# An adaLN block with attention on one Trainium2 core: the second query group made first, the modulation rows moved behind

## The chip, the core and the metric

The kernel runs on one core of a Trainium2 chip. The metric is the device time of one execution in microseconds (us); lower is better. The core has a matrix engine (TensorE, PE below), a vector engine (VectorE, DVE), a scalar engine (ScalarE, ACT), a general engine (GpSimd, POOL), an engine that starts transfers (SyncE, SP), and queues for transfers (DMA). Each engine works off its own list of instructions in order; where one needs another engine's result, it waits on a semaphore.

## What is computed

The sequence has 2048 rows of 512 columns. There are 32 heads of 16 columns for the queries, and one key and one value head that all of them share.

```python
def _A_ref(x, wq, wk, wv, wo):
    q = (x @ wq).reshape(B, S, H, Dh).transpose(0, 2, 1, 3)
    k, v = x @ wk, x @ wv
    scores = jnp.einsum("bhqd,bkd->bhqk", q, k) * (Dh ** -0.5)
    o = jnp.einsum("bhqk,bkd->bhqd", softmax(scores), v)
    return o.transpose(0, 2, 1, 3).reshape(B, S, H * Dh) @ wo

x = A_x
sa, ca, ga, sb, cb, gb = split_in_six(silu(c) @ w_mod)
h = layernorm(x) * (1 + ca) + sa
x = x + ga * _A_ref(h, A_wq, A_wk, A_wv, A_wo)
h = layernorm(x) * (1 + cb) + sb
x = x + gb * (gelu(h @ w1 + b1) @ w2 + b2)        # 1376 columns in between
```

Everything is float32, and the result must be close to float32 products. The kernel therefore splits each operand into a high part (fp32r, a type that PE multiplies in one pass) and the remainder as a low part, and makes three products for one: high by high, low by high and high by low.

## The kernel before

The rows are worked in four blocks of 512. For a block the prologue takes the statistics of the rows (`stats1`), normalizes them on ACT (`xhat1`, L362), turns each of four column parts of 128 with PE's transposes into a tile `tp` (`turn1`, L371), applies scale and shift on ACT (`mod1`, L377) and splits the result into `h0H`/`h0L` for block 0 and `big1H`/`big1L` to `big3H`/`big3L` for the others (L134 or L132 the high, L139 the low part). These four steps of a column part are called a head of the block below. Then come the products for keys and values, `kps` (L164, twelve of them, since there are four column parts k and three products each); ACT copies the keys into `ks` (L392) and the values into `vt` (L393), DVE makes the keys' low part (`low_k`, L398), ACT repeats it on other partitions (`repeat_k`, L402), and PE turns the values (`v_out`, `vps`, L410).

Queries come in four groups of 128 columns. `prep_wq(g)` splits the weight of group g, in two halves j of the columns, into the tiles `wqH` and `wqL`, each of which holds all 512 columns of the four parts k (ACT's copy L334, POOL's subtraction L335). `qproj(b, g)` makes the group's twelve products `qps` (mm3, L164), three for each k, takes the high and low part out of them and sends both to memory (`send_q`, L415); `load_q(u)` (L487 and L488) reads them back in another layout into a tile `qst`, for a unit u of the attention. Group 0 of block 0 feeds the units 0 and 1, group 1 the units 2 and 3.

The softmax needs the maximum of each row of scores first. `Max.step` makes a product m of `qst` and `ks` on PE (L517), 512 keys wide, and DVE reduces it (L522). A unit has 32 of these products in four sets of keys kc, and the table FIRST_MAX says in which order the sets of the units 0 and 1 are taken: set kc can be made when block kc's keys are ready. When the last reduction of unit 0 is done, `put_max` reduces over the sets (`mm`, L571), turns the result (L572), gathers it on POOL (`mt`, L566), splits it, and transfers it into rows of `qst` (L561). Then the first product e of unit 0 runs (L597), the second product of the same scores, now less the maximum, then the exponential on ACT (L598) and the products with the values (L609).

The order of the code is the order on each engine. In the prologue's last part it is set by the table SLOTS: each entry makes so many max products and then one step of each piece of work that it names ("keys 1" is one k of block 1's key products, "heads 2" a head of block 2, "low 1" `low_k` of block 1, "k 1" `repeat_k`, "v 0" `v_out`, "q 1" a k of group 1's projection, "wq 1" `prep_wq(1)`, "rows" a fourth of the late modulation rows `modl`, L289, and "load" the query loads of unit 2). The rest of the modulation (`modr`) is made at the start. Past the table a loop makes the attention, one unit behind the other; the order from the first e on is set by the planner that is not touched here. While the projection of group 0 is made, `stats1(2)` runs on DVE, and a function `first_q` that is called between its parts makes the projection.

## Times and profile before

| | us |
|---|---|
| median of three runs (1581.46 to 1582.77) | 1582.67 |
| the profiled execution | 1580.99 |
| its span, first to last instruction | 1579.2 |
| PE busy in it | 1556.4 |
| DVE busy | 1405.5 |
| ACT busy | 1204.6 |
| POOL busy | 694.9 |
| the first max product of unit 0 | 33.16 |
| the first product e of unit 0 | 78.47 |

The span is the time from the first instruction to the last, and the profiled execution's own time lies 1.8 above it. Busy time is a sum over all stages; which stage an engine limits is seen in a timeline. A line of a timeline has the start and the duration of an instruction or of a run of equal ones ("x3"), its engine, line, operation and tiles (out<-in), and in brackets the idle time before it and what ended it. The granted clock (PEclk) is a share of 2.4 GHz: 1.00 is 2.4 GHz, 0.50 is 1.2 GHz.

### The profile page before, as it was taken

Reading aid. Unit: us, or ns where it says so; the run is one execution under the profiler, and the core shown is the slowest. Engines: PE = TensorE matmul, PEld = TensorE weight load, DVE = VectorE, ACT = ScalarE, POOL = GpSimd, SP = SyncE. Lnnn points to the kernel's source line nnn. Section 1 sums busy time; section 2 is a strip of 40 time slices with the busy share of each in tenths; the row PEclk is TensorE's granted clock in tenths of the full one; section 3 lists DMA queues with packets and bytes.
Section 4 is the critical chain, followed back from the end, with each engine's and each line's share of the span. In section 5 each row is a group of like instructions: output and inputs, shape, how many; then the busy total and the mean of one; then the engine's idle time right before and its main releaser. Section 6 shows DMA issues by size and latency. Waiting matters only on the chain.

```text
span 1579.2 us, 43484 instructions
## 1 busy us (share of the span) xinstructions
PE 1556.4 (99%) x17514; PEld 1040.6 (66%) x17514; DVE 1405.5 (89%) x2491; ACT 1204.6 (76%) x2418; POOL 694.9 (44%) x1253
## 2 busy tenths in 40 slices
PE   5999999999999999999999999999999999999999
PEld 3466655667766676667766676666766677676767
DVE  7899999999999999999999999999999999999715
ACT  5577777788777887778877887778877788778853
POOL 4445457447422472245623363334712464324731
PEclk8999999999999999999999999999999999999999
DMA  7135322313021220302112120212112130221231
GB/s 261 73 108 205 118 83 89 99 44 97 21 61 62 64 78 21 101 25 95 45 54 72 45 98 20 92 33 85 56 36 89 36 109 22 60 80 50 96 141 54
DMA packets 80859, 121.48 MB, mean 77 GB/s; under 512 B 16187, under 2 KB 55355, under 8 KB 80401
## 3 DMA queue, kind: packets, MB, share of 16 engines
q1 hardware_dynamic: 80640, 118.70, 23.1%
q8 instruction: 137, 2.24, 0.6%
q14 instruction: 66, 0.53, 0.1%
q10 hardware_dynamic: 16, 0.00, 0.0%
HBM read 91.00 MB, written 26.88 MB: 75 GB/s over the span
## 4 chain that ended last, share of the span: by engine, by line
PE 95%; ACT 3%; DVE 1%; DMA 1%; issue 0%; POOL 0%; SPq 0%; DVEq 0%; ACTq 0%
PE acc L609 32%; PE e L597 20%; PE m L517 19%; PE w1ps L193 8%; PE w2ps L193 6%; PE wops L193 3%; PE qps L193 2%; ACT p L598 2%; PE w2ps L187 1%; PE w1ps L187 1%; DMA xt<-in_A_x_dram 1%; PE tp L193 1%; PE kps L164 1%; DVE mx L522 1%; PE wops L187 0%
## 5 line engine op out<-in xcount | busy, mean ns | idle before, releaser
L522 DVE TENSOR_REDUCE mx<-m 128x1 f32<-128x512 f32 x2048 | 1271.5, 682 | 98.2 <-PE m L517 87.4
L598 ACT ACTIVATE p<-e 128x512 f32<-128x512 f32 x2048 | 1067.2, 601 | 291.5 <-PE e L597 204.2
L517 PE MATMUL m<-ks,qst 64*128 64x512 f32 x2048 | 829.2, 432 | 6.0 <-DVE mv L203 4.6
L597 PE MATMUL e<-qst,ks 64*128 64x512 f32 x2048 | 731.8, 412 | 2.1 <-ACT wqH L334 1.3
L609 PE MATMUL acc<-p,va 128*32 128x256 f32 x8192 | 548.8, 385 | 0.0
L517 PEld LDWEIGHTS m<-ks,qst 64*128 64x128 f32 x2048 | 367.3, 184 | 103.2 <-DVE mx L522 83.5
L597 PEld LDWEIGHTS e<-qst,ks 64*128 64x128 f32 x2048 | 357.7, 184 | 112.6 <-ACT p L598 102.0
L609 PEld LDWEIGHTS acc<-p,va 128*32 128x32 f32 x8192 | 214.0, 109 | 217.6 <-issue 113.9
L193 PE MATMUL w1ps<-h2H,w1t 64*128 64x256 f32 x1232 | 236.2, 288 | 0.0
L193 PEld LDWEIGHTS w1ps<-h2H,w1t 64*128 64x128 f32 x1232 | 184.0, 184 | 31.7 <-issue 22.2
L566 POOL TENSOR_SCALAR mt<-turned 8x32 f32<-8x32 f32 x256 | 53.1, 208 | 342.1 <-DVE turned L572 330.0
L193 PE MATMUL w1ps<-h2L,w1t 64*128 64x256 f32 x616 | 169.3, 275 | 0.0
L193 PE MATMUL w2ps<-w2H,gH 64*128 64x256 f32 (+1 forms) x556 | 162.2, 296 | 0.0
L193 PE MATMUL w2ps<-w2L,gH 64*128 64x256 f32 (+1 forms) x556 | 156.5, 283 | 0.0
L193 PE MATMUL w2ps<-w2H,gL 64*128 64x256 f32 (+1 forms) x556 | 155.1, 283 | 0.0
L193 PEld LDWEIGHTS w1ps<-h2L,w1t 64*128 64x128 f32 x616 | 113.5, 184 | 0.0
L193 PEld LDWEIGHTS w2ps<-w2H,gH 64*128 64x128 f32 x556 | 101.6, 184 | 10.7 <-issue 4.9
L193 PEld LDWEIGHTS w2ps<-w2H,gL 64*128 64x128 f32 x556 | 101.8, 184 | 2.3
L193 PEld LDWEIGHTS w2ps<-w2L,gH 64*128 64x128 f32 x556 | 102.4, 184 | 1.2
L965 POOL TENSOR_SCALAR tt<-tt 128x256 f32<-128x256 f32 x77 | 31.0, 403 | 145.1 <-ACT tt L964 144.8
L193 PE MATMUL wops<-woH,onH 64*128 64x256 f32 x224 | 67.9, 303 | 0.0
L193 PE MATMUL wops<-woL,onH 64*128 64x256 f32 x224 | 62.2, 278 | 0.0
(235 smaller groups left out, 1604.6 us busy)
## 6 DMA issues: line engine op xcount, KB each, us to landing
w1t<-dw SPq DMA_DIRECT2D x82, 512.0 KB
qst<-dq SPq DMA_DIRECT2D x128, 64.0 KB
do<-oc SPq DMA_DIRECT2D x63, 128.0 KB
dw<-w1s SPq DMA_DIRECT2D x11, 512.0 KB
xt<-in_A_x_dram SPq DMA_DIRECT2D x4, 1024.0 KB
dq<-qH SPq DMA_DIRECT2D x16, 256.0 KB
dq<-qL SPq DMA_DIRECT2D x16, 256.0 KB
qst<-dq SPq DMA_DIRECT2D x128, 32.0 KB
```

The costliest lines, as they stand in the source:

```text
L164: nc.tensor.matmul(ps, a, b_, start=begin and n == 0, stop=end and n == last)
L187: nc.tensor.matmul(ps, a, b_, start=first_, stop=last_)
L193: nc.tensor.matmul(ps, a[rows], b_[rows], start=first_ and s == begin, stop=last_ and s != begin)
L517: nc.tensor.matmul(m, qsts[u][rows, j, t * P:(t + 1) * P], ks[rows, kc * 512:(kc + 1) * 512], start=True, stop=True)
L522: nc.vector.tensor_reduce(out=self.mx[u][:, i, kc:kc + 1], in_=m, axis=AX.X, op=ALU.max)
L566: nc.gpsimd.tensor_scalar(out=mt[:, g:g + 32], in0=turned[g:g + 4 * T, :], scalar1=1.0, scalar2=0.0, op0=ALU.mult, op1=ALU.add)
L597: nc.tensor.matmul(e, ks[rows, kt * P:(kt + 1) * P], rhs, start=True, stop=True)
L598: nc.scalar.activation(ptiles[u, K][:, j, s, :], e, AF.Exp, scale=0.25)
L609: ins = nc.tensor.matmul(accs[u][32 * cidx:32 * cidx + 32, :], va[:, kt, :], rhs, start=kt == 0, stop=kt == NKT - 1)
L965: nc.gpsimd.tensor_scalar(out=tt, in0=tt, scalar1=1.0, scalar2=1.0, op0=ALU.mult, op1=ALU.add)
```

## The change

`prep_wq` takes an engine for the high part, and now leaves the split to `split`: group 0 goes as before, by ACT and POOL, while for the groups 1 to 3 both parts are made on POOL (a TENSOR_SCALAR, L132, and the subtraction, L139, for each half). `prep_wq(1)` is called right after the first two instructions of block 1's normalizing, ahead of `first_q` in the code. Group 1's projection (`q_group`) is called behind `repeat_k(0)`, ahead of the normalizing of blocks 2 and 3 and of the first max product. In SLOTS the weights of groups 2 and 3 are made at other places, the steps of "q 1" are gone, the first step of "keys 3", which had no max products with it, has two, and the four parts of "rows" stand in the last four entries with "load" in the first of these; "v 2" and "v 3" have entries with two max products each, and two entries have max products alone.

```diff
 SLOTS = (...,
-         (2, "low 2", "k 2", "v 1", "wq 1"), (0, "keys 3"), (2, "keys 3"), (2, "keys 3"), (2, "keys 3"), (2, "low 3", "k 3"),
-         (0, "v 2"), (2, "q 1"), (2, "q 1"), (2, "q 1"),
-         (2, "q 1", "rows"), (2, "v 3", "load", "wq 2", "wq 3"), (2, "rows"), (2, "rows"), (2, "rows"))
+         (2, "low 2", "k 2", "v 1", "wq 2"), (2, "keys 3"), (2, "keys 3"), (2, "keys 3"), (2, "keys 3", "wq 3"), (2, "low 3", "k 3"),
+         (2, "v 2"), (2, "v 3"), (2, ), (2, ),
+         (2, "rows", "load"), (2, "rows"), (2, "rows"), (2, "rows"))
...
-    def prep_wq(g):
+    def prep_wq(g, eng=nc.gpsimd):
         gs = slice(g * P, (g + 1) * P)
         for j in range(2):
...
-            nc.scalar.copy(dh, src)
-            nc.gpsimd.tensor_tensor(out=dl, in0=src, in1=raw(dh), op=ALU.subtract)
+            split(dh, dl, src, eng, nc.gpsimd)
...
-    prep_wq(0)
+    prep_wq(0, act)
...
     rows = xhat1(1, act)
     run(rows, 2)
+    prep_wq(1)
...
     repeat_k(0)
+    run(q_group())
     run(xhat1(2, act))
     run(xhat1(3, act))
-    work = {..., "q 1": q_group(), ..., "wq 1": one(prep_wq, 1), "wq 2": one(prep_wq, 2), "wq 3": one(prep_wq, 3)}
+    work = {..., "wq 2": one(prep_wq, 2), "wq 3": one(prep_wq, 3)}
```

On PE, the beginning of group 0's projection in the program before; the brackets name the engines whose semaphores the instruction waits for:

```order
L164 MATMUL qps_0_314<-h0H,wqH 128x512 [waits Activation_49]
L164 MATMUL qps_0_314<-h0H,wqL 128x512 [waits Pool_49]
L164 MATMUL qps_0_314<-h0L,wqH 128x512 [waits Pool_49]
L164 MATMUL qps_0_314<-h0H,wqH 128x512 [waits Pool_49]
L164 MATMUL qps_0_314<-h0H,wqL 128x512
L164 MATMUL qps_0_314<-h0L,wqH 128x512 [waits DVE_49]
```

The same place on PE in the program after:

```order
L164 MATMUL qps_0_318<-h0H,wqH 128x512 [waits Activation_49]
L164 MATMUL qps_0_318<-h0H,wqL 128x512 [waits Pool_49]
L164 MATMUL qps_0_318<-h0L,wqH 128x512 [waits Pool_49]
L164 MATMUL qps_0_318<-h0H,wqH 128x512 [waits Pool_49]
L164 MATMUL qps_0_318<-h0H,wqL 128x512 [waits Pool_49]
L164 MATMUL qps_0_318<-h0L,wqH 128x512 [waits DVE_49]
```

The products and their order are the same; the fifth, which had no wait, has one for POOL.

On POOL, from the low part of block 0's first column part on, in the program before:

```order
L139 TENSOR_TENSOR h0L<-h_0_0_258,h0H 128x512 [waits Activation_49]
L132 TENSOR_SCALAR h0H<-h_0_1_275 128x512 [waits Activation_49]
L207 TENSOR_TENSOR rs<-ve,mhalf 128x4 [waits DVE_49]
L352 TENSOR_TENSOR nm_292<-mv,rs 128x4 [waits Pool_49]
L353 TENSOR_SCALAR nm_292<-nm_292 128x4 [waits Pool_49]
L266 MEMSET b1c 128x1
L207 TENSOR_TENSOR rs<-ve,mhalf 128x4 [waits DVE_49]
```

The same stretch of POOL in the program after:

```order
L207 TENSOR_TENSOR rs<-ve,mhalf 128x4 [waits DVE_49]
L351 TENSOR_TENSOR nm_292<-mv,rs 128x4 [waits Pool_49]
L352 TENSOR_SCALAR nm_292<-nm_292 128x4 [waits Pool_49]
L266 MEMSET b1c 128x1
L132 TENSOR_SCALAR wqH<-wqf 128x4x64 [waits DMAHW2_49]
L139 TENSOR_TENSOR wqL<-wqf,wqH 128x4x64 [waits Pool_49]
L132 TENSOR_SCALAR wqH<-wqf 128x4x64
L139 TENSOR_TENSOR wqL<-wqf,wqH 128x4x64 [waits Pool_49]
L207 TENSOR_TENSOR rs<-ve,mhalf 128x4 [waits DVE_49]
```

The four instructions of group 1's split stand between the memset of `b1c` and the statistics of block 2.

On ACT, from the last head of block 1 to the copy of block 1's keys, in the program before:

```order
L134 CAST big1H<-h_1_3_420 128x512 [waits Activation_49]
L402 CAST ks<-ks 16x512 [waits DVE_49]
L362 ACTIVATE xt_148<-xt_148,nm_351,rs 128x512 [waits DMAHW3_49,Pool_49]
L362 ACTIVATE xt_148<-xt_148,nm_351,rs 128x512 x3
L362 ACTIVATE xt_151<-xt_151,nm_432,rs 128x512 [waits DMAHW5_49,DVE_49,Pool_49]
L362 ACTIVATE xt_151<-xt_151,nm_432,rs 128x512 [waits DVE_49] x3
L392 CAST ks<-kps_459 48x512 [waits PE_49]
```

The same stretch of ACT in the program after:

```order
L134 CAST big1H<-h_1_3_424 128x512 [waits Activation_49]
L401 CAST ks<-ks 16x512 [waits DVE_49]
L440 COPY q_0_1_457<-qps_1_442 128x512 [waits PE_49,Pool_49]
L134 CAST qH_1_455<-q_0_1_457 128x512 [waits Activation_49]
L361 ACTIVATE xt_148<-xt_148,nm_355,rs 128x512 [waits DMAHW3_49]
L361 ACTIVATE xt_148<-xt_148,nm_355,rs 128x512 x3
L361 ACTIVATE xt_151<-xt_151,nm_436,rs 128x512 [waits DMAHW5_49,DVE_49,Pool_49]
L361 ACTIVATE xt_151<-xt_151,nm_436,rs 128x512 [waits DVE_49] x3
L391 CAST ks<-kps_484 48x512 [waits PE_49]
```

The copy and the cast of group 1's query stand ahead of the normalizing of blocks 2 and 3.

## Rows read from the trace of the kernel before

**Rows 1.** The page: the span, and the chain that ended last, by engine.

```profile
span 1579.2 us, 43484 instructions
...
PE 95%; ACT 3%; DVE 1%; DMA 1%; issue 0%; POOL 0%; SPq 0%; DVEq 0%; ACTq 0%
```

**Rows 2.** Timeline of PE, 18.5 to 38 us: start, duration, engine, line, operation.

```profile
19.00 0.50 PE L164 MATMUL qps<-h0L,wqH 128*128 128x512 f32 x1
19.59 0.50 PE L164 MATMUL qps<-h0H,wqH 128*128 128x512 f32 x1
...
24.56 0.39 PE L164 MATMUL kps<-h0L,wkH 128*128 128x512 f32 x1
...
33.16 1.19 PE L517 MATMUL m<-ks,qst 64*128 64x512 f32 x3 [4.57 <-DVE mv L203]
...
35.43 0.79 PE L164 MATMUL kps<-big1H,wkH 128*128 128x512 f32 x1
...
36.87 0.63 PE L164 MATMUL kps<-big1H,wkH 128*128 128x512 f32 x1
37.30 0.63 PE L164 MATMUL kps<-big1H,wkL 128*128 128x512 f32 x1
```

**Rows 3.** Timeline of SP's queue, 20 to 30 us.

```profile
24.77 0.34 SPq L415 DMA_DIRECT2D dq<-qL  x1
```

**Rows 4.** Busy time of engines by half microsecond; the granted clock stands behind POOL.

```profile
29.50:30.00 0.50, 0.00 (x0) 0.00 (x0) 0.50 (x2) 0.47 (x2) 0.50 (x2) 0.71 0.35 107
30.00:30.50 0.50, 0.00 (x0) 0.00 (x0) 0.30 (x1) 0.50 (x2) 0.47 (x1) 0.50 0.13 41
39.00:39.50 0.50, 0.50 (x3) 0.49 (x2) 0.39 (x1) 0.00 (x0) 0.00 (x0) 0.50 0.97 393
...
40.00:40.50 0.50, 0.50 (x4) 0.42 (x3) 0.40 (x1) 0.00 (x0) 0.00 (x0) 1.00 1.18 483
```

**Rows 5.** Timeline of ACT, 21 to 46; a group of 0 to 80.

```profile
23.45 0.56 ACT L437 CAST qH<-qps 128x512 fp32r<-128x512 f32 x1
...
25.33 1.16 ACT L392 CAST ks<-kps 48x512 fp32r<-48x512 f32 x2
...
31.88 0.62 ACT L402 CAST ks<-ks 16x512 fp32r<-16x512 f32 x1
32.53 5.75 ACT L362 ACTIVATE xt<-xt,nm,rs 128x512 f32<-128x512 f32 x8
41.12 1.17 ACT L392 CAST ks<-kps 48x512 fp32r<-48x512 f32 x2 [2.85 <-PE kps L164]
...
L441 ACT COPY q<-qps 128x512 f32<-128x512 f32 x1 | 0.6, 585 | 4.1 <-PE qps L164 4.1
```

**Rows 6.** Timeline of DVE, 24 to 46 us.

```profile
33.96 2.48 DVE L522 TENSOR_REDUCE mx<-m 128x1 f32<-128x512 f32 x4 [0.49 <-PE m L517]
```

**Rows 7.** Timelines of PE and then of DVE, 61 to 80 us.

```profile
62.09 0.39 PE L164 MATMUL kps<-big3L,wkH 128*128 128x512 f32 x1
...
75.64 1.06 PE L289 MATMUL modl<-wml,csb 128*32 128x512 f32 x8
...
78.47 0.59 PE L597 MATMUL e<-qst,ks 64*128 64x512 f32 x2 [1.33 <-ACT wqH L334]
...
64.31 0.68 DVE L398 TENSOR_TENSOR ks<-kps,ks 16x512 fp32r<-16x512 f32 x1
...
72.73 0.19 DVE L571 TENSOR_REDUCE mm<-mx 128x8 f32<-128x32 f32 x1
```

**Rows 8.** POOL: timeline, 8 to 27; groups, 0 to 80; the page.

```profile
21.92 0.10 POOL L266 MEMSET b1c<- 128x1 f32 x1
...
L335 POOL TENSOR_TENSOR wqL<-wqf,wqH 128x256 fp32r<-128x256 f32 x8 | 5.8, 758 | 9.8 <-ACT wqH L334 9.8
...
L132 POOL TENSOR_SCALAR h0H<-h 128x512 fp32r<-128x512 f32 x1 | 0.6, 617 | 0.0
...
L965 POOL TENSOR_SCALAR tt<-tt 128x256 f32<-128x256 f32 x77 | 31.0, 403 | 145.1 <-ACT tt L964 144.8
```

More of the change, by code (lines that the diff above doesn't have):

```diff
@@ L1322, in adaln_mqa_mlp @@
     repeat_k(0)
+    run(q_group())
     run(xhat1(2, act))
     run(xhat1(3, act))
-    work = {"keys 1": keys(1), "heads 2": heads(2), "heads 3": heads(3), "q 1": q_group(), "keys 2": keys(2), "keys 3": keys(3),
+    work = {"keys 1": keys(1), "heads 2": heads(2), "heads 3": heads(3), "keys 2": keys(2), "keys 3": keys(3),
             "v 0": one(v_out, 0), "v 1": one(v_out, 1), "v 2": one(v_out, 2), "v 3": one(v_out, 3), "rows": late_rows(),
             "low 1": one(low_k, 1), "low 2": one(low_k, 2), "low 3": one(low_k, 3), "k 1": one(repeat_k, 1), "k 2": one(repeat_k, 2), "k 3": one(repeat_k, 3), "load": one(load_q, 2),
-            "wq 1": one(prep_wq, 1), "wq 2": one(prep_wq, 2), "wq 3": one(prep_wq, 3)}
+            "wq 2": one(prep_wq, 2), "wq 3": one(prep_wq, 3)}
     for n, *names in SLOTS:
```

## The prediction

> **What bounds the kernel now.** The page comes first: one execution spans 1579.2 us, and the chain that ended last is 95% TensorE (PE) [rows 1]. After the first e product, at 78.47 us, PE hardly waits, and from that instruction on the two programs give every engine the same order. So the edit is worth what it does to the time of the first e; a shift there goes to the end. I therefore read the timelines of 18 to 80 us, PE first, and then, for each instruction of PE, what it waits for.
>
> Three things are to be seen. First, group 0's twelve query products run as a chain: the third starts at 19.00, the fourth at 19.59, and the twelve products of block 0's keys behind them end at 24.56 + 0.39 = 24.95 [rows 2]. At full clock such products come 0.25 us apart on the mean (twenty steps from 19.59 to 24.56). Second, PE then has little to do until the first max product at 33.16, whose query goes through memory: the low half is sent at 24.77, and the product starts 8.4 us later [rows 2, 3]. In that hole the granted clock goes to 0.71 at 29.50 and 0.50 at 30.00, that is from 2.4 to 1.2 GHz, and it is back at 1.00 at 40.00 [rows 4]; key products of block 1 inside it are 0.43 apart (36.87, 37.30) [rows 2]. Third, ScalarE (ACT) is a chain too: it copies group 0's query at 23.45, the keys at 25.33, makes block 1's heads, repeats the keys at 31.88, then normalizes blocks 2 and 3 for 5.75 us until 38.28, waits 2.85 us, and copies the next keys at 41.12 [rows 5]. From there the max products and the reductions of VectorE (DVE), 0.62 each [rows 6], set the pace to the last reduction of unit 0, which the reduction mm follows at 72.73 and the first e 5.74 later [rows 7].
>
> **The change part by part.** *The weight of group 1 on GpSimd (POOL), early.* It becomes four POOL instructions behind the memset of 21.92 [rows 8], each half a TENSOR_SCALAR and a TENSOR_TENSOR. The second kind took 758 ns at this very line. The first is not in the trace in this form: a 128x256 one took 403, a 128x512 one 617 [rows 8]. I take 0.405, the same size, and get 22.02 + 2 x (0.405 + 0.758) + 0.1 of gaps = 24.45; with 0.62 it is 24.9. The third instruction ends at about 23.65, the fourth at 24.45.
>
> This would be free if only group 1 read it. The order of the changed program says otherwise: the second h0H,wqL product of group 0 now waits for POOL, where it had no wait, and the h0H,wqH before it waits for POOL as well; followed to their producers, those waits are for the third and the fourth instruction of the new split, not for h0H alone as before. Groups are columns of one tile with four k rows each, so the stretch from the first to the last byte that group 1 writes includes group 0's columns of k = 1 to 3, and the dependence is drawn on that stretch. Program order makes it worse: the split is written before the projection, and so the projection waits. Only the three products of k = 0 escape.
>
> *The price of that wait.* PE stops at 19.00 + 0.50 = 19.5 [rows 2] and goes on with one product at about 23.9 and the rest from 24.8 (a little semaphore time included). Nineteen products are left behind it in its queue, seven of group 0 and twelve of the keys; group 0's end moves from 22.21 to 26.6 at full clock. But PE has then stood for 4.3 to 5 us, and in the trace, where PE stood for 4.57 us ahead of 33.16, the clock was at 0.50 from 30.00 on [rows 2, 4]. So I expect the 1.2 GHz level when it resumes: 0.43 per product, group 0 out at about 28.65 (24.8 + 8 x 0.43, and what the last one takes beyond its spacing). I take full clock again at about 29.5, as far behind the start as 40.00 stands behind the start of block 1's key products at 35.43, or at 31.6, if it is counted from 33.16 [rows 2, 4]. The keys then end at 31.9 (30.9 to 32.5) instead of 24.95; at full clock throughout they would end at 29.5 (24.8 + 19 x 0.25).
>
> "TensorE: Matmul & The Clock Gate" of the Trainium skill, in "What's actually happening", calls the throttled state the default and says that activity releases it. The trace agrees in direction: 0.50 after the hole, 1.00 after work [rows 4]. By that rule alone the end of group 0 may find the clock released already, and the sum would be about 1 us less.
>
> *What is queued behind it.* ACT's qH copy waits for the projection, 23.45 to about 28.65 (+5.2); the keys' copy follows at 32.0 instead of 25.33 (+6.7). The heads of block 1, DVE's low part and the repeat of keys follow in the same order, so the repeat ends at 31.88 + 0.62 + 6.7 = 39.2.
>
> *Group 1's projection moved to before the max products.* Its twelve products fit into PE's new wait for the query (the first max product at 33.16 + 5.2 = 38.4), and cost PE nothing there. On ACT they cost a copy of 585 ns and a cast like the 0.56 at 23.45 [rows 5] ahead of the normalizing: 1.2 with the gaps. Its low part is one subtraction on POOL, at most twice the 758 ns, where POOL waits for the heads of block 2, which come behind the copy of 41.12; its two sends, 0.34 each [rows 3], pass one weight load in SP's queue, and unit 2 that reads them is far off: nothing for either. The normalizing of 5.75 then ends at 39.2 + 1.2 + 5.75 = 46.15 where it ended at 38.28. In the kernel before 2.85 us of idle time came behind it [rows 5]; that cover is used up: block 1's key products, which ended at about 41.1, end 6.2 later with DVE's first reduction (33.96 goes with the heads, to 40.15) less 0.2 for each of nine to twelve that now run at full clock, at 44.9 to 45.5 [rows 2, 6], so ACT is late next and the copy of 41.12 starts at about 46.15. Shift: 6.7 + 1.2 - 2.85 = +5.05, with 4.0 to 5.65 by the two bounds of the keys' end.
>
> *Slots.* From there the pattern is that of before, DVE at its pace, until the last key products. PE loses twelve query products there, and the slot ahead of block 3's keys that held no max products now holds two, so that these keys end 2 x 0.62 = 1.25 later. Behind that end, before: mm 72.73, keys 62.09 + 0.39 = 62.48, 10.25 us. After: low part 1.85 us behind the keys' end as before (64.31) and 0.68 long [rows 7], ACT's repeat and first product 0.7, then 8 reductions of 0.62, 8.2 us. Together 1.25 + 8.2 - 10.25 = -0.8; rounded down for a gap of PE between them, -0.75.
>
> *Modulation rows behind unit 0.* All four groups, 1.06 each [rows 7], now run after unit 0's last max product, in the 5.74 us in which its maxima go through POOL and memory. Four of them, eight max products of 0.5 and gaps end about 0.25 before the first e could start; three were there before. They cost nothing, and if one more microsecond came they would. So the gain of the tail is 0.75 at most with the first e 0.03 later: 0.72. The weights of groups 2 and 3, now on POOL, are eight instructions, about 4.7 us, in POOL's idle time ahead of unit 0's gather: nothing. ACT loses their casts where it was not bound; nothing too. Neither case has a row of its own; the bound of both is a gain or a loss of some 0.6, one reduction of DVE.
>
> Sum: +5.05 - 0.72 = +4.3 us. On the profiled execution, 1580.99 us, that is 1585.3; this execution was 1.7 below the median of the runs, 1582.67, so I give the forecast on the median: 1582.67 + 4.3 = 1587.0.
>
> **The rivals.** *A: the wait comes, the clock stays up.* For it: the hole of before lay behind short transposes, this one lies behind dense products and has one in it. Against it: it is as long. Then the keys end at 29.5, their copy is +4.5 (+4.3 with less of a gap), the shift 4.4 + 1.2 - 2.85 = 2.75, less 0.72: +2.0, 1584.7, and 1584.1 with the reduction less: no change that can be measured.
>
> *B: the low clock lasts into block 1's keys.* The work between, heads of short transposes, may not raise it. Then block 1's keys run as in the trace, where most of them were at 0.43, and end with DVE's first reduction 6.2 to 6.7 later; the shift is that, and with 6.6 less 0.72 it is +5.9, 1588.6. For it: in the trace the clock stayed at 0.50 from 30.00 to 39.50 though max and key products ran from 33.16 [rows 2, 4]. "PE-mode transpose" in the same page of the Trainium skill says that transposes do not count as busy in the same way; nothing in the trace before separates that from their shortness.
>
> *C: the wait does not hold the projection.* The change would then do what its words say: group 1's weight and products lie in holes, group 0 is as before, the normalizing ends at 38.28 + 1.2 = 39.5, and block 1's keys at full clock (group 1's products have filled the hole) some 1.8 before 41.1, so that the copy of 41.12 comes 1.6 earlier. That gives -1.6 - 0.72 = -2.3, with one reduction more or less -1.7 to -2.9: about 1580.4, faster. It decides from the point at which the split ends before 19.6. Against it: behind the memset the split starts at 22.02 [rows 8], and the wait stands in the built order.
>
> **How the numbers follow.** Forecast (wait and low clock) 0.66, A 0.12, B 0.18, C 0.04. A measurement of this kernel tells about 0.2%, 3.2 us, from no change: 1579.5 to 1585.8. The forecast's own range is 1586.0 to 1587.6 by the shift (4.0 to 5.65), 1585.4 to 1588.2 with the reduction more or less; it and B are slower but for its lower end, 0.12, which is the same with A; C is faster. So faster 0.04, same 0.24, slower 0.72. The range goes from A's 1584.1 to B's 1588.6 with most of a reduction above: 1584.1 to 1589.0.
>
> **What would show it.** Right, if PE's row of group 0 shows a gap of 4 to 5 us behind its third product with POOL's split as releaser, a granted clock of 0.50 in the next microseconds, ACT's key copy near 32 instead of 25.33, block 1's key copy near 46 instead of 41.12, and the first e near 82.8. A is right if the clock row there stays at 1.00, B if products of block 1's keys are 0.43 apart, C if group 0's products still come 0.2 to 0.4 apart. The forecast is wrong too if the max products of unit 0 end earlier than DVE's pace says, or if the first e waits for PE's modulation rows.

## The result, and the profile of the changed kernel

The changed kernel takes 1590.78 us (median of five, 1586.22 to 1595.25), the kernel before 1582.67 in the same comparison (1580.37 to 1582.77). The ratio is 1.0050, with a 95% interval of 1.0036 to 1.0065. Measured a second time (e15 below), it was 1589.69 against 1582.06. So it is slower by some 8 us, where +4.3 was foretold and 1589.0 was the upper end.

The page of the profiled execution, the lines that answer to [rows 1]; this execution is 9.8 us longer than that of before:

```profile
span 1589.0 us, 43483 instructions
...
PE 1562.9 (98%) x17514; PEld 1044.4 (66%) x17514; DVE 1404.0 (88%) x2491; ACT 1202.5 (76%) x2412; POOL 697.9 (44%) x1259
...
PE 94%; ACT 3%; DVE 1%; DMA 1%; issue 0%; POOL 0%; SPq 0%; ACTq 0%; DVEq 0%
```

PE's timeline from 18 to 50 us, the columns as in [rows 2]:

```profile
18.52 0.50 PE L164 MATMUL qps<-h0L,wqH 128*128 128x512 f32 x1
23.17 0.79 PE L164 MATMUL qps<-h0H,wqH 128*128 128x512 f32 x1 [4.15 <-POOL wqH L132]
...
27.57 0.63 PE L164 MATMUL kps<-h0H,wkH 128*128 128x512 f32 x1
...
30.63 0.39 PE L164 MATMUL kps<-h0L,wkH 128*128 128x512 f32 x1
...
46.26 0.50 PE L516 MATMUL m<-ks,qst 64*128 64x512 f32 x1
48.30 0.49 PE L516 MATMUL m<-ks,qst 64*128 64x512 f32 x1 [1.55 <-DVE mx L521]
```

The wait for the split is there. PE stands (is idle) for 4.15 us behind group 0's third product, and the line names POOL's `wqH` (L132) as its end; the products behind it are 0.43 apart until 28.4 (27.57 is the first of block 0's keys), and those keys end at 30.63 + 0.39 = 31.02 where before they ended at 24.95. A second stand, of 1.55 us, lies between two max products at 46 to 48 us; before it was 0.57 there. ACT's timeline, 21 to 54 us, against [rows 5]:

```profile
31.06 1.17 ACT L391 CAST ks<-kps 48x512 fp32r<-48x512 f32 x2 [1.25 <-PE kps L164]
...
39.41 5.75 ACT L361 ACTIVATE xt<-xt,nm,rs 128x512 f32<-128x512 f32 x8
45.07 1.16 ACT L391 CAST ks<-kps 48x512 fp32r<-48x512 f32 x2
```

The copy of block 1's keys comes at 45.07, 3.95 later than the 41.12 of before, and right behind the normalizing: ACT has no idle time ahead of it any more. Then DVE: the low parts of the keys of blocks 1, 2 and 3 (L397) and mm (L570):

```profile
46.84 0.68 DVE L397 TENSOR_TENSOR ks<-kps,ks 16x512 fp32r<-16x512 f32 x1 [1.06 <-ACT vt L392]
...
65.77 0.68 DVE L397 TENSOR_TENSOR ks<-kps,ks 16x512 fp32r<-16x512 f32 x1
...
73.16 0.68 DVE L397 TENSOR_TENSOR ks<-kps,ks 16x512 fp32r<-16x512 f32 x1
...
80.53 0.18 DVE L570 TENSOR_REDUCE mm<-mx 128x8 f32<-128x32 f32 x1
```

Before, these four stood at 42.91, 58.22, 64.31 and 72.73; the last two are in [rows 7], the first two are

```profile
42.91 0.68 DVE L398 TENSOR_TENSOR ks<-kps,ks 16x512 fp32r<-16x512 f32 x1
...
58.22 0.68 DVE L398 TENSOR_TENSOR ks<-kps,ks 16x512 fp32r<-16x512 f32 x1
```

So the lateness goes +3.93, +7.55, +8.85, +7.80. It nearly doubles between blocks 1 and 2, where I had put nothing. The granted clock (behind POOL's busy time, as in [rows 4]) over the stretches that matter:

```profile
22.50:28.00 5.50, 4.80 (x11) 3.43 (x12) 0.00 (x0) 0.73 (x2) 1.35 (x3) 0.50 0.28 51
29.00:48.50 19.50, 14.66 (x69) 9.84 (x67) 13.78 (x31) 17.95 (x29) 7.91 (x11) 1.00 0.67 231
49.50:59.00 9.50, 9.50 (x35) 5.93 (x36) 6.72 (x11) 6.55 (x11) 7.79 (x9) 0.50 0.32 115
60.00:72.50 12.50, 11.44 (x43) 5.64 (x43) 11.60 (x19) 4.18 (x8) 6.08 (x13) 1.00 0.00 1
73.50:85.50 12.00, 11.60 (x38) 4.52 (x38) 8.31 (x15) 1.04 (x3) 1.78 (x7) 0.50 0.02 4
87.50:89.00 1.50, 1.50 (x12) 0.34 (x10) 1.24 (x2) 0.16 (x1) 0.00 (x0) 1.00 0.73 197
```

There are three stretches at 0.50: from the wait to 28.7, from 49 to 59.5, and from 73 to 87. Before, there was one from 29.5 to 40, and one from 80.5 to 84.5, behind the first e. PE's timeline shows what the second and the third do (the line of 70.94 is the last of block 3's key products):

```profile
50.22 1.11 PE L370 MATMUL tp<-ident,xt 128*128 128x128 f32 x4
...
51.83 0.80 PE L516 MATMUL m<-ks,qst 64*128 64x512 f32 x2
...
70.94 0.39 PE L164 MATMUL kps<-big3L,wkH 128*128 128x512 f32 x1
...
73.90 1.44 PE L516 MATMUL m<-ks,qst 64*128 64x512 f32 x2 [2.14 <-DVE ks L397]
...
77.12 3.56 PE L516 MATMUL m<-ks,qst 64*128 64x512 f32 x6
80.61 1.93 PE L289 MATMUL modl<-wml,csb 128*32 128x512 f32 x8
...
88.66 0.50 PE L596 MATMUL e<-qst,ks 64*128 64x512 f32 x2
```

At half clock a head's four transposes take 1.11 us and two max products 0.80, so that a slot takes PE 1.77 (51.83, 53.60 and so on), where DVE needs 1.25 for its two reductions. And the first two groups of modulation rows take 1.93 each, the third 1.52, instead of 1.06: the first e stands behind four groups, 8.13 us behind mm instead of 5.74. Ahead of the line of 73.90 PE stood 2.14 us for block 3's low keys, and the clock fell within this stand, at 73. Before, two more max products and then group 1's projection lay there.

### The profile page after: what moved, and what is told of

Its sections match the earlier page's. It is cut to its first block, busy times and chain, and to the rows that moved or that the text cites. A ratio compares the mean times of both kernels' runs of the same rounds, so it can differ in the third digit from the quotient of the medians.

```text
span 1589.0 us, 43483 instructions
## 1 busy us (share of the span) xinstructions
PE 1562.9 (98%) x17514; PEld 1044.4 (66%) x17514; DVE 1404.0 (88%) x2491; ACT 1202.5 (76%) x2412; POOL 697.9 (44%) x1259
## 4 chain that ended last, share of the span: by engine, by line
PE 94%; ACT 3%; DVE 1%; DMA 1%; issue 0%; POOL 0%; SPq 0%; ACTq 0%; DVEq 0%
PE acc L608 32%; PE e L596 19%; PE m L516 18%; PE w1ps L193 8%; PE w2ps L193 6%; PE wops L193 3%; PE qps L193 2%; ACT p L597 2%; PE w2ps L187 1%; PE w1ps L187 1%; DMA xt<-in_A_x_dram 1%; PE tp L193 1%; DVE mx L521 1%; PE kps L164 1%; PE wops L187 0%; PE modl L289 0%
```

## The experiments

All were timed in five rounds beside the kernel before on the same chip. Where the column "before" is empty, the value above it holds, from the same runs. Medians in us:

| run | what it is | median | before | ratio (95%) |
|---|---|---|---|---|
| e1_layout | change without the wait | 1583.76 | 1583.22 | 1.0005 (0.9994 to 1.0015) |
| e2_hold_warm | change, wait filled | 1588.48 | | 1.0030 (1.0018 to 1.0041) |
| e3_split_early | before, with the early split | 1586.80 | | 1.0022 (1.0014 to 1.0030) |
| e4_late_warm | change, two later stands filled | 1588.41 | | 1.0043 (1.0028 to 1.0057) |
| e5_layout_fill | e1, heavy filling at its end | 1588.80 | 1581.65 | 1.0044 (1.0030 to 1.0057) |
| e6_layout_rows | e1, rows spread | 1587.26 | | 1.0038 (1.0025 to 1.0052) |
| e7_before_fill | before, first stand filled | 1580.60 | | 0.9994 (0.9985 to 1.0003) |
| e8_all_warm | change, heavy filling everywhere | 1592.29 | | 1.0066 (1.0043 to 1.0089) |
| e9_layout_fill2 | e1, light filling at its end | 1583.04 | 1582.96 | 1.0005 (0.9996 to 1.0013) |
| e10_all_warm2 | change, light filling everywhere | 1587.38 | | 1.0022 (1.0013 to 1.0032) |
| e11_before_fill2 | before, both stands filled | 1579.94 | | 0.9982 (0.9974 to 0.9991) |
| e12_layout_fill3 | e9, first stand filled too | 1579.65 | | 0.9985 (0.9976 to 0.9994) |
| e13_layout_keys3 | e1, keys of block 3 as before | 1581.30 | 1582.06 | 0.9992 (0.9983 to 1.0001) |
| e14_fifth_warm | change, fifth slot filled | 1586.23 | | 1.0034 (1.0022 to 1.0046) |
| e15_after_again | change | 1589.69 | | 1.0041 (1.0029 to 1.0053) |
| e16_layout_q2 | e1, group 2 in the empty slots | 1587.41 | | 1.0032 (1.0021 to 1.0043) |
| e18_layout_best | e13, light filling | 1578.00 | 1583.11 | 0.9966 (0.9954 to 0.9978) |
| e19_hold_alone | e18 with the wait | 1582.81 | | 0.9995 (0.9987 to 1.0004) |

**Is it the wait, and is the link false?** e1 changes no order and no instruction, only where a group's weight lies in its tile, so that the bytes of group 1 no longer span those of group 0:

```diff
-    wqH = att.tile([P, KD, D], F32R, name="wqH", tag="gH")
-    wqL = att.tile([P, KD, D], F32R, name="wqL", tag="gL")
+    wqH = att.tile([P, KD, KD, P], F32R, name="wqH", tag="gH")
+    wqL = att.tile([P, KD, KD, P], F32R, name="wqL", tag="gL")
...
-        return [(wqH[:, k, gs], wqL[:, k, gs], hH[:, k, :], hL[:, k, :]) for k in range(KD)]
+        return [(wqH[:, g, k, :], wqL[:, g, k, :], hH[:, k, :], hL[:, k, :]) for k in range(KD)]
```

> The changed kernel with one edit: the weight tiles wqH and wqL are laid out group by group, so that the bytes of group 1 no longer span those of group 0; every engine's order stays. Theory (the link through the tile's address range holds group 0's projection, and the lateness that follows is what costs): the products of group 0 come 0.2 to 0.5 us apart again, the copy of block 1's keys is at about 39.5 where it was 45.07, and the 1.55 us of standing ahead of the second max product of 46 us is under 0.8. The 2.1 us of standing behind block 3's keys stays, for the slots make it, and with it a fallen clock under the modulation rows: time between -2 and +2 us of the kernel before. Rival (POOL's split or the slots cost by themselves): +4 us or more.

PE's timeline of e1 from 18 to 22 us, and from 27 to 45:

```profile
18.81 0.50 PE L164 MATMUL qps<-h0L,wqH 128*128 128x512 f32 x1
19.40 0.50 PE L164 MATMUL qps<-h0H,wqH 128*128 128x512 f32 x1
19.73 0.40 PE L164 MATMUL qps<-h0H,wqL 128*128 128x512 f32 x1
```

```profile
30.75 0.40 PE L164 MATMUL qps<-h0L,wqH 128*128 128x512 f32 x1
34.34 0.70 PE L516 MATMUL m<-ks,qst 64*128 64x512 f32 x3 [3.19 <-DMA qst<-dq]
```

The wait is gone and with it nearly all of the loss: the link was one of addresses, not of data. But the copy of block 1's keys did not come at 39.5. It came at 41.19, since PE stood again ahead of the first max product (3.19 us, for the query's transfer) and the clock fell from 36 to 40. And it fell a second time, for 20 us:

```profile
36.50:39.50 3.00, 3.00 (x9) 1.62 (x7) 0.82 (x2) 2.71 (x4) 0.00 (x0) 0.50 1.02 369
...
60.50:80.00 19.50, 17.40 (x51) 7.42 (x51) 13.41 (x23) 2.77 (x6) 2.13 (x11) 0.50 0.01 1
```

So the change without its wait is no better than before.

e3 is the other half: the early split alone in the kernel before (`prep_wq(1, nc.gpsimd)` behind `run(rows, 2)`, "wq 1" out of SLOTS).

> The kernel before with the split of group 1's weight alone moved: made by GpSimd, early, as in the change; projection of group 1, slots and rows stay as before. Theory: group 0's projection stands 4 us for the split, the clock falls there and again ahead of the first max product, and the copy of block 1's keys comes 3 to 5.5 us later than 41.12; the projection of group 1 in the late slots keeps PE fed, so there is no long standing near 72 us: +3 to +5.5 us. Rival (the wait is hidden behind ACT's 2.85 us of idle time): within 1 us of before.

+3.6 us, as expected; its trace has the wait (3.85 us), a stand of 4.41 before the first max product, block 1's keys copied 5.6 later (46.75), and no long stand after that. The wait alone is thus 3.6, the rest alone 0.5, and both together 8. The sum is missing 4.

**What the clock costs.** For this I let PE work on products that nothing reads (`warm`), where it stands; each writes into a bank, one of the buffers that take PE's results, and `tags` names the banks, which are taken in turn; in e2, in the wait for the split:

```diff
+    def warm(n, *tags):
+        for i in range(n):
+            tag = tags[i % len(tags)]
+            ps = psum.tile([P, BQ], F32, name=f"idle{len(idles)}", tag=tag, bufs=3 if tag == "m" else 1)
+            nc.tensor.matmul(ps, wkH[:, 0, :], wkH.rearrange("p k n -> p (k n)"), start=True, stop=True)
...
-            run(q_group())
+            for i, _ in enumerate(q_group()):
+                if i == 0:
+                    warm(18, "m")
```

> The changed kernel with 18 products of no use in PE's wait for the split (after the first three of group 0's projection). Theory (the wait is one price, the low clock behind it another of about 1.9 us, and the two later falls of the clock are a third): granted clock 1.00 from 19 to 31 us, block 0's keys copied near 29.3 instead of 31.06, and 1.5 to 2.5 us less than the changed kernel, that is +5 to +7 against before if the later falls stay. Rival (the low clock in the wait is most of the loss): +3 us or less.

Block 0's keys were copied at 29.52, 1.5 earlier than in the changed kernel, and the clock was 1.00 there; +5.3 us by the medians. It fell later all the same (47.5 to 54.5, 64.5 to 85.5), so the wait's own low clock is the smaller part. e4 filled the two later stands (six products in the fifth slot, on the bank "x", nine behind block 3's keys):

> The changed kernel with products of no use in the two later places where PE stands: six between the two max products of the fifth slot (46 to 48 us), nine behind block 3's low keys (71 to 74 us). Theory (the clock that falls behind these two costs some 3.6 and 2.4 us, of the 8 to 10 lost): granted clock 1.00 from 46 to 60 and from 71 to 88 us, modulation rows 1.06 each instead of 1.93, and +3 to +5 us against before. Rival (the clock there is a companion of the lateness, the pace is DVE's anyhow): +7 us or more, as the change.

The result lies between the two. In the profiled execution the clock stayed at 1.00 from 46 to 76.5, and the low parts of blocks 1 and 2 were 16.7 apart instead of 18.9; but then it fell from 77 to 84.5, where PE had only max products at DVE's pace, and the first e still stood 8.03 behind mm, behind groups of rows at 1.93, 1.93 and 1.42. Filling the stand was not enough; the clock also fell in the thin slots behind it. Three of the eleven executions took 1593.7 to 1596.6, the others 1587.2 to 1588.7.

**Two fillings that were too heavy.** e5 and e8 put products into the slots that the projection of group 1 had left.

```diff
+    for i, (n, *names) in enumerate(SLOTS):
         chunk(n)
+        if len(SLOTS) - 9 <= i < len(SLOTS) - 5:
+            warm(9 if i == len(SLOTS) - 9 else 3, "v")
```

> The changed kernel with the weight laid out group by group (no hold) and with products of no use where the projection of group 1 stood before: nine behind block 3's last key products, three in each of the next three slots. Theory (the moved projection was what kept the clock up between block 3's keys and the first e product; without it PE gets only max products at VectorE's pace, the clock falls, and the modulation rows at 1.93 us each end behind the maxima): clock 1.00 from 68 to 78 us, modulation rows near 1.06, the first e product less than 6.5 us behind mm, and -0.5 to -2 us against the kernel before, 1.5 to 3 less than the layout alone. Rival (rows are too late in the order at any clock): same as the layout alone, +0 to +1.

> The changed kernel as it is, wait for the split included, with products of no use in the wait, between the two max products of the fifth slot, behind block 3's keys and in the next three slots. It leaves only the wait itself. Theory: clock 1.00 from 19 to 80 us, block 0's keys copied at about 29.5, block 1's at 43.5, mm 1 to 2 us later than 72.73, and +1 to +2.5 us against before, so that three quarters of the loss of the change are the clock's. Rival (the wait is the loss): +4 us or more.

Both fail, by my own doing. PE's timeline of e5, 56 to 100 us:

```profile
67.50 4.92 PE L290 MATMUL idle<-wkH 128*128 128x512 f32 x9
...
72.78 1.61 PE L290 MATMUL idle<-wkH 128*128 128x512 f32 x3
```

All these products write one bank, each waits for the end of the one before it, and one takes 0.54 us instead of 0.24: nine are 4.92 us in a hole of 2.1. They say nothing on the theory; mm came 13.3 us behind block 3's low keys instead of 8.4, and e8 adds the wait to that.

e6 filled these slots with two of the four groups of rows:

```diff
-         (2, "v 2"), (2, "v 3"), (2, ), (2, ),
-         (2, "rows", "load"), (2, "rows"), (2, "rows"), (2, "rows"))
+         (2, "v 2"), (2, "v 3", "rows"), (2, "rows"), (2, ),
+         (2, "load"), (2, "rows"), (2, ), (2, "rows"))
```

> The changed kernel with the weight laid out group by group, and the four groups of modulation rows spread: two in the slots ahead of unit 0's last max products, where the projection of group 1 stood before, two behind them, with a slot between. Theory: the rows are work in the place of useless products and are off the way of the first e product at either clock: first e 5.8 to 6.3 us behind mm, and -0.5 to -2 us against before. Rival (two groups are too little to keep the clock up, and it falls as in the layout alone; DVE's pace then is 1.0 us per slot slower): +0 to +2.

The rival held, and the result is worse than it said (+5.6): the stand behind block 3's keys stays (2.14), the clock falls at 69.5, before the rows begin, and stays down to 87. The two groups at 1.93 each are then ahead of unit 0's last maxima instead of behind them.

**Light filling.** e9, e10 and e12 take three banks in turn (0.24 to 0.36 a product), fewer products, and, e12, twelve ahead of the first max product: `fills = {len(SLOTS) - 9: 8, len(SLOTS) - 8: 2, len(SLOTS) - 7: 2, len(SLOTS) - 6: 3}`, on the banks "e0", "e1", "e2".

> As the run that filled the slots of group 1's former projection, layout group by group, but with the useless products on three banks in turn, so that one takes 0.24 us and not 0.54, and fewer of them: eight behind block 3's last key products, two, two and three in the next slots. Theory (the clock that falls where PE gets only max products is what makes the modulation rows late): clock 1.00 from 68 to 80 us, rows 1.06 each, the first e 5.5 to 6.5 us behind mm, and 0 to -2 us against before, at least 1 us under the layout alone. Rival (the fall comes earlier, in block 3's keys, and filling behind it is of no use): as the layout alone, 0 to +2, first e over 7 us behind mm.

> The changed kernel, layout group by group, twelve useless products ahead of the first max product behind group 1's projection, and the light filling behind block 3's keys. Theory (the change as it was meant, without the hold and without the falls of the clock): the copy of block 1's keys at 39.3 to 39.8, mm at about 70.5 to 71, the first e 5.5 to 6.5 behind it, -2 to -3.5 us against before. Rival (the falls come anyway, or the rows are late): 0 or slower.

> The changed kernel, wait for the split included, with the same light filling: 18 products in the wait, four ahead of the first max product, three between the two of the fifth slot, and the fifteen behind block 3's keys. It leaves the wait itself. Theory: no fall of the clock in the first 80 us, the copy of block 1's keys at 43.0 to 43.8 instead of 41.12, mm at most 2.5 us later, and +1 to +2.5 us against before. Rival (the wait itself is the loss): +4 us or more.

e9, PE's timeline behind block 3's keys, the last group of rows and the first e (mm is at 77.46):

```profile
68.28 2.12 PE L290 MATMUL idle<-wkH 128*128 128x512 f32 x8
...
81.78 1.06 PE L296 MATMUL modl<-wml,csb 128*32 128x512 f32 x8
83.21 0.62 PE L603 MATMUL e<-qst,ks 64*128 64x512 f32 x2 [0.36 <-DMA qst<-ml]
```

There is no fall between 56 and the first e, the rows take 1.06 each, and the first e is 5.75 behind mm, as expected; but the clock fell at 35 and 48.5 ahead of that, so that the time was that of e1 (+0.1) and not 1 us under it. e12 had no fall in the profiled execution (granted clock 1.00 from 18 to 80), its copy of block 1's keys at 39.39, the first e at 77.25: -3.3 us by the medians, -1.5 per thousand by the ratio. That is the change as it was meant. Its executions also show the price of the clock within one kernel: the six whose mean granted clock was 0.999 or 1.000 took 1578.4 to 1579.7, the five at 0.996 to 0.998 took 1582.3 to 1583.2. e10, with the wait, was +4.4 by the medians, the number of its rival; but its trace still had falls at 39 and 62.5, which the theory had excluded. Three of its eleven executions had a mean granted clock of 1.000, and these took 1583.5 to 1584.3, that is +0.5 to +1.3, at or just under the theory's lower end.

Fillings in the kernel before, with none of the change; the first line stands in e7 and e11, the second in e11 alone:

```diff
+    warm(18, "m")
     for n, *names in SLOTS:
...
+    warm(2, "v")
     while mp.done < lead[0]:
```

> The kernel before with 18 products of no use in the 4.6 us in which PE waits for the first query. Theory (the low clock of the kernel before, 29.5 to 40.0, delays block 1's key products and through them the chain of ACT and DVE): clock 1.00 throughout, the copy of block 1's keys at 39.5 to 40 instead of 41.12, -1 to -1.6 us. Rival (the query's transfer and DVE's reductions set the pace there): within 0.5 us of before.

> The kernel before with 18 useless products in PE's wait for the first query and two more ahead of the first e product. Theory (the falls of the clock from 29.5 and from 80.5 are each a price of their own in the kernel before): -1.5 to -2.5 us. Rival (the second fall is covered by DVE's and ACT's pace): as with the first filling alone, -1 us.

e7: the copy of block 1's keys at 39.51 instead of 41.12, the first e 1.5 earlier, and the clock falls only behind the first e (79 to 82.5); -1.0 us, with an interval that just includes no change. e11 has no fall at all and -3.0 us. So useless products alone give the kernel before what e12 gives the changed one: with the clock up, the early projection and the moved rows are worth nothing measurable in the order of e12.

**Why the two halves cost more together.** e15 is the changed kernel again; e14 fills only the stand in the fifth slot (three products on the bank "x" between its two max products).

> The changed kernel itself, for comparison on this chip. Theory and rival: +6 to +10 us against before, with falls of the clock behind the hold, in the heads of blocks 2 and 3 and in the modulation rows, not all in every execution.

> The changed kernel, hold included, with three useless products between the two max products of the fifth slot. Theory (the hold makes ACT late, ACT makes the keys' low part late, PE stands 1.55 us, the clock falls and PE takes 1.77 us per slot where DVE needs 1.25): clock 1.00 from 46 to 60 us, the low parts of blocks 1 and 2 about 15.5 us apart and not 18.9, and 2 to 4 us under the changed kernel. Rival (the fall comes by chance, not from that stand): within 1.5 us of the changed kernel.

e15's trace repeats that of the result: a stand of 1.54 ending at 48.20, the clock down from 49.0 to 59.5, the low parts of blocks 1 and 2 18.93 apart. In e14:

```profile
46.00:60.00 14.00, 13.88 (x67) 8.02 (x66) 12.00 (x19) 11.92 (x19) 9.81 (x9) 1.00 0.48 174
...
66.00:86.00 20.00, 17.90 (x52) 7.58 (x51) 13.75 (x24) 2.77 (x6) 2.29 (x11) 0.50 0.00 1
```

No fall there, and the low parts are 16.02 apart, 2.9 less. But in this execution the clock was down from 42 to 45 as well, and DVE's low part did not wait for ACT; e19 below is the cleaner test of this stage. The whole is less plain too: 3.5 us less by the medians, but the ratios' intervals overlap, and this execution has a fall of 20 us behind it. The mechanism, as the changed kernel's trace has it, is: the wait makes ACT late (its idle time of 2.85 is used up, as [rows 5] let expect, by 1.2 of the new copies and the lateness), DVE's low part waits for ACT, PE runs out of banks for max products and stands 1.55, the clock falls, and a stage that DVE paced is paced by PE, at 1.77 a slot (2.47 for the slot that also turns values), until 59.

e13 puts the first step of block 3's keys back without max products, with a slot more before the rows:

```diff
-         ..., (2, "keys 3"), (2, "keys 3"), (2, "keys 3"), (2, "keys 3", "wq 3"), (2, "low 3", "k 3"),
-         (2, "v 2"), (2, "v 3"), (2, ), (2, ),
+         ..., (0, "keys 3"), (2, "keys 3"), (2, "keys 3"), (2, "keys 3", "wq 3"), (2, "low 3", "k 3"),
+         (2, "v 2"), (2, "v 3"), (2, ), (2, ), (2, ),
```

> The changed kernel with the weight laid out group by group, and the first step of block 3's keys again without max products, as in the kernel before; their two max products get a slot of their own before the rows. Theory (two max products at VectorE's pace ahead of those keys leave PE thin there, and the clock falls in them): clock 1.00 from 58 to 66 us, low part of block 3's keys 6.1 us behind that of block 2, the fall behind these keys stays, and 0 to 1.5 us under the layout alone, -1 to +0.5 against before. Rival (that fall has nothing to do with the slot): as the layout alone, 0 to +1.5.

Block 3's low keys came 6.06 behind block 2's, at full clock, and the stand of 2.1 behind them shrank to 0.50, for there were max products left to make. -0.8 us against before by the medians, where the layout alone had +0.5 on another chip. The fall behind these keys (68 to 78.5) stayed, as foretold. Why the clock fell near 60 us in e1, e5 and e10, where PE had stood no longer than 0.32 us, is not settled by one trace without it.

e16 is the attempt to fill the slots with work that counts, group 2 of the same block (a "q 2" in four slots):

> The changed kernel with the weight laid out group by group, and with block 0's projection of group 2 made in the slots where that of group 1 stood before: twelve products that the attention loop need not make. Theory (work in the emptied slots keeps the clock up, and PE, which bounds the loop, has twelve products of 0.23 less there): no fall behind block 3's keys, first e under 6.5 us behind mm, and -2 to -4.5 us against before. Rival (the query's copies on ACT and POOL get in the way of unit 0's maxima, or the loop's plan doesn't use the room): -0.5 to +2.

It failed, +5.4 us, worse than its rival. The clock fell at 61.5 and at 72; with twelve products more in these slots, at half clock each at 0.43, PE needs 2.3 us a slot there. And the twelve products that the loop no longer makes bought nothing: from the first e to the end it is 1500.3 us, as in the changed kernel, and 1500.7 before.

**The wait by itself.** e18 is e13 with light filling, e19 the same with the weight laid out as in the change:

> The changed kernel with the weight laid out group by group, the first step of block 3's keys without max products, twelve useless products ahead of the first max product, and two or three in each of five slots from block 3's keys on. Theory: no fall of the clock up to the first e product, the copy of block 1's keys at 39.3 to 39.9, mm at 70.5 to 72, the first e 5.7 behind it, -2 to -4 us against before. Rival (the filled slots or the slot more are in DVE's way): -1 or slower.

> The same with the weight laid out as in the change, so that group 0 waits for the split, with eighteen useless products in that wait, four ahead of the first max product and three in the fifth slot. It differs from e18 by the wait and by ACT's lateness behind it. Theory: no fall of the clock, block 0's keys copied at 29.0 to 29.6, block 1's at 43.0 to 43.8 (3.5 to 4 later than in e18), and 3.5 to 4.5 us over e18, that is about 0 to +1.5 against before. Rival (the wait is worth more by itself, or falls come anyway): +3 against before or more.

The granted clock of e18, then of e19:

```profile
18.00:50.00 32.00, 29.38 (x138) 19.79 (x137) 26.02 (x54) 30.29 (x48) 20.97 (x27) 1.00 0.71 238
50.00:80.00 30.00, 29.30 (x137) 13.62 (x139) 27.14 (x46) 11.22 (x22) 10.63 (x22) 1.00 0.09 23
```

```profile
18.00:50.00 32.00, 29.08 (x132) 19.99 (x132) 21.86 (x48) 26.89 (x41) 17.13 (x24) 1.00 0.60 206
50.00:80.00 30.00, 29.36 (x138) 14.20 (x137) 27.98 (x46) 11.25 (x22) 14.56 (x25) 1.00 0.12 38
```

Neither has a fall. PE's timeline of e19 at the wait, ACT's copies of block 1's keys in e19 and in e18, and the first e of e19 and of e18:

```profile
19.72 4.28 PE L290 MATMUL idle<-wkH 128*128 128x512 f32 x18
23.83 0.42 PE L164 MATMUL qps<-h0H,wqH 128*128 128x512 f32 x1
24.58 0.50 PE L164 MATMUL qps<-h0H,wqL 128*128 128x512 f32 x1 [0.33 <-POOL wqL L139]
```

```profile
43.49 1.15 ACT L398 CAST ks<-kps 48x512 fp32r<-48x512 f32 x2
```

```profile
39.55 1.17 ACT L398 CAST ks<-kps 48x512 fp32r<-48x512 f32 x2
```

```profile
79.88 0.59 PE L603 MATMUL e<-qst,ks 64*128 64x512 f32 x2 [0.33 <-DMA qst<-ml]
```

```profile
75.95 0.59 PE L603 MATMUL e<-qst,ks 64*128 64x512 f32 x2 [0.33 <-DMA qst<-ml]
```

DVE's low parts of the keys of blocks 1 and 2 in e19:

```profile
45.26 0.68 DVE L404 TENSOR_TENSOR ks<-kps,ks 16x512 fp32r<-16x512 f32 x1 [1.03 <-ACT vt L399]
...
60.54 0.68 DVE L404 TENSOR_TENSOR ks<-kps,ks 16x512 fp32r<-16x512 f32 x1
```

The copy is 3.94 later in e19 than in e18, the first e 3.93 later: at full clock the wait costs about 4 us, and it goes through ACT to the first e unchanged. The time is 4.8 longer by the medians; the last 0.9 lies behind the first e and is not explained. DVE's low part waits for ACT as in the changed kernel (1.03 here, 1.06 there), but with the clock up the low parts are 15.28 apart, as they were before (15.31), and not 18.93. So the lateness of ACT does not stretch that stage; the low clock does. That is shown.

The two prices do not simply add up. Against before, e19 is -0.3: with the clock up, even the wait leaves no loss. With the wait, the falls of the clock cost about 7 us (the changed kernel +8.1, e10's three executions at full clock +0.5 to +1.3); without it, about 4 (e1 +0.5, e12 -3.3). Turned round, the wait costs 4 to 5 where the clock stays up and 7.6 in the changed order where it can fall (e1 against the changed kernel). The kernel before pays about 3.0 for falls of its own (e11).

Without wait and falls, e18 is 5.1 us faster than before (0.9966) and by far the steadiest: its seven times lie within 1.3 us, the five of the change within 9.0. Some 4 of the 5 us are the clock's: e11, the kernel before with its two stands filled, has 1578.4 to 1580.0 in its executions at a mean clock of 1.000, e18 has 1577.5 to 1578.8. The difference, about 1 us, would be the change's own, but the two ran on different chips, so that it is not shown. e18 is the version to keep of those tried, and it still holds 25 products that nobody reads.

## Where the prediction was right and where it failed

In the profiled executions the first e came 10.2 us later (88.66 for 78.47), where the sum had 4.3. By its terms: 1.1 less than foretold up to the copy of block 1's keys, 3.6 more in the heads behind it, 1.0 more in the last slots, 2.4 more in the modulation rows.

*The wait:* right. That the built program made group 0's second triple wait for the split could be read ahead of the run, the place (third product), the releaser and the length (4.15, foretold 4.4 for the first product) are those of the trace. e1 shows that the link is one of addresses.

*The clock behind it:* right in kind, sized a little too dear. 0.50 was there when PE resumed, all that was left of group 0 was made at it, and 1.00 came back near 28.8 (I had taken 29.5). Group 0's copy came 4.35 later (foretold 5.2), the keys' copy 5.73 (6.7). In part that is because this execution began 0.5 us earlier (18.52 for 19.00).

*ACT's cover used up:* right. The copy of block 1's keys stands directly behind the normalizing; +3.95, foretold +5.05 with 4.0 as its lower end, so that it lies just under it. Up to this point I had lost too much, not too little.

*"From there the pattern is that of before, DVE at its pace":* this is the step that failed. It was a sentence without a row, and it was wrong by 3.6 us between the low parts of blocks 1 and 2 (18.93 apart, before 15.31). I had made the lateness of ACT the term, but had not asked what PE does in the meantime: it makes the max products that it has banks for and stands. The slots hold for DVE's pace only at full clock; the same slot costs PE 1.77 at half. At full clock the sentence holds: in e19, with ACT as late, the two are 15.28 apart. Rival B had the clock down in block 1's keys; it was not down there, but in the heads behind them.

*The modulation rows "cost nothing":* the second step that failed, by 2.4 us. I had written that they would cost if one more microsecond came, and gave them 1.06 each, from a stretch at full clock (1.00 from 60 to 80 us in the kernel before). At half clock they take up to 1.93; with the clock up they do cost nothing (e9: 1.06 each, the first e 5.75 behind mm). The 2.1 us of standing behind block 3's keys could have been read from the order: the first step of "keys 3" now takes two max products, so that two fewer are left behind these keys, and the next product is a max product that needs the keys which DVE and ACT are still making. e13 puts the two back, and the stand is 0.50; but the clock falls there all the same. That group 1's projection in these slots was what kept the clock up in the kernel before is argued and not shown: useless products in its place keep it up (e9), the projection of group 2 in its place did not (e16).

*The slots' own gain:* a third miss, of 1.0 us. The low part of block 3 came 1.30 later relative to block 2's (foretold 1.25), which is right. But from the end of block 3's key products (70.94 + 0.39 = 71.33) to mm it is 9.20 us, where 8.2 was foretold and 10.25 was measured before. So the slots lost 0.25 where they were to gain 0.75. DVE did not work off its eight reductions there without a gap, as the sum had it: it waited twice for max products (0.88 and 0.59), at half clock. What full clock alone would have given is not shown, since the runs that have it there have useless products in these slots.

*The bounds:* the range had one reduction of DVE, 0.6, for everything that I had no row for. The clock's phase was the largest unknown and stood only in the rivals A and B, each with one stretch. The spread of the change's own times, 9.0 us, shows that it belonged in the range.

*Rival A:* its condition, the wait at full clock, is met in e19 and in three executions of e10, by useless products: -0.3 and +0.5 to +1.3, where it had +2.0. The changed kernel by itself did not keep its clock.

*Rival C:* its condition, no wait, is e1. It gave +0.5 by the medians, not -2.3, for the same reason. With the clock kept up (e12) it is -3.3, but the first e is only 1.2 earlier (77.25 for 78.47); the rest is not accounted for.

## What to carry to other kernels

A dependence may be drawn on the stretch of bytes from the first to the last that an instruction touches: before a piece of a shared tile is written earlier than its readers of other pieces, look at the waits of the built program, or lay the pieces out one behind the other.

When work is moved out of a thin stretch, ask what the matrix engine does there now, and price the stretch at both levels of its clock: a schedule that another engine paces at 2.4 GHz may be paced by the matrix engine at 1.2. If the times of a kernel spread much more than those of another one, that is the sign to look for, and the mean granted clock of each execution shows it (e12).

## What the runs showed of the hardware

The granted clock went from 1.00 to 0.50 behind a stand of PE of 1.55 us (until 48.30 in the changed kernel, the fall at 49), within a stand of 2.14 us (until 73.90, the fall at 73), and also where it had not stood longer than 0.5 us but had only max products at DVE's pace to make (68 us in e13, 77 us in e4); I had looked for falls behind the two long stands only. "TensorE: Matmul & The Clock Gate" of the Trainium skill says in "PE-mode transpose" that transposes do not count as busy in the same way. Here the heads between 41 and 51 us of the kernel before, transposes and max products in turn, ran at 1.00 throughout; in e9 and e13 the clock fell in the same mix (at 49 and 48), behind the same short stand of PE (0.57 and 0.56). So these runs neither show a part of the transposes in the falls nor exclude one.

Products that write the same PSUM bank one behind the other took 0.54 us each at full clock, in three banks in turn 0.24 to 0.27 (e5: nine in 4.92; e2: 18 in 4.25; e9: eight in 2.12).
